# The opening of a fused Fourier transform and feed-forward kernel: one table in another queue, x ahead of w1, fewer warm-ups, weight loads behind the first relayout

## The chip, the core and the metric

The kernel runs on one core of a Trainium2 chip. The core has a matrix engine (PE, with its weight loads listed as PEld), a vector engine (DVE), a scalar engine (ACT), a general engine (POOL) and a sync engine (SP) that issues most of the transfers. ACT and POOL can issue transfers too. Each engine works through its own instructions in order; semaphores between them tell when a tile is ready. Sixteen DMA engines move the data between device memory and the core's SBUF.

The metric is the time of one execution on the device in microseconds (us), lower is better.

## What is computed

```python
def _attn_ref(x):                       # x: (8, 3136, 256), float32
    X = np.fft.fft(x, axis=1)
    X = np.fft.fft(X, axis=2)
    return X.real.astype(np.float32)

def _moe_ref(x, g_ln, w_ch1, w_ch2):    # w_ch1: (256, 1024), w_ch2: (1024, 256)
    mu = np.mean(x, axis=-1, keepdims=True)
    var = np.mean((x - mu) ** 2, axis=-1, keepdims=True)
    xn = (x - mu) / np.sqrt(var + 1e-06) * g_ln
    ch = np.maximum(xn @ w_ch1, 0.0) @ w_ch2
    return (x + ch).astype(np.float32)

# out = _moe_ref(_attn_ref(x), ...)
```

x is float32. The weights w_ch1 and w_ch2 arrive as 64-bit floats, which the kernel reads as pairs of 32-bit words and turns into 32-bit floats itself.

## The kernel before

The 3136 positions of a batch are split as 49 x 64. Per batch, **step1** is the transform over the 64: seven pieces (`step1(b, i)`), each a matmul group against the table tu (`tu_s`) on tiles that were folded into sums first (`fold_zw`, on DVE for batch 0). `step1_ends` does the columns that the fold leaves out; it reads `ends` (POOL). Each piece is copied out of PSUM by ACT (L267) and stored to scratch in device memory (`store1`, L271). When all seven pieces of a batch are stored, **relayout** (L278) reads them back with the 49 on the partitions; batch 0 does so in three parts (groups 0 to 4, 4 to 8, 8 to 16). **step2** (L311) is the transform over the 49, against the table tab (`tab_s`) and, for the first group, tz (`tz_s`). ACT casts its result to the rounded high part ckh (L332), DVE makes the low part ckl (L336).

Then come 49 chunks of 256 positions with their mirror images, 8 steps each: `moe1_a` (matmuls with w1, L356, and sum and difference on ACT and DVE, L361 to L363), `moe1_b` (ReLU and split into high and low part, L370 and L371) and `moe2` (matmuls with w2, L406). Each product is made of three passes of rounded high and low parts. The transform over the 256 columns is folded into w1 (`transform_w1`, L576) in the opening, and the residual goes through its own small matmuls (L431).

The weights are converted in pieces. Four pieces of w1 (w1_0 to w1_3) and four of w2 share the same four buffers: `load_w2(n)` writes where w1_n was, so it comes after the conversion of w1_n has read it. A conversion has an ACT part, `convert_z` (L531), and DVE parts, `convert_m` (L523, L525) and `convert_b` (L536, L538); `convert_b` needs both. `finish_w1` (L566) and `finish_w2` (L598) put the parts together; `split_w2` makes high and low part of w2 (ACT L542, POOL L543); `round_w1` (L584) and `rest_w1_copy` (L594), both on ACT, make those of w1.

The order of the work of PE, ACT, DVE and POOL, and in the opening of SP too, is the order of the lines from L685 on: every engine takes its own instructions in the order in which they stand there. In the opening ACT has, behind the step1 copies, `convert_z` of the w1 pieces, the two casts of `round_w1(0)`, `convert_z` of w2_0 and of w2_1, `rest_w1_copy(0)`, `round_w1(1)`, the cast of `split_w2(0)` and then the ckh casts of step2. PE has step1, the transforms of w1, fifteen warm-up matmuls, step2 for the first two pairs of groups and then `moe1_a(0)`. The eight warm-ups at the very start (L683, L691) multiply zeros; three of them are in float32, which PE runs as two passes each, and five in bfloat16.

The transfers of one engine form one queue, and a semaphore of a small set tells when a transfer has landed. An issue also waits until the transfer that used its semaphore before has landed.

Of the kernel before, what the change touches and what calls it, by code (L numbers as in the profile page):

```python
# [146 lines left out]
def tile_kernel(ctx: ExitStack, tc: tile.TileContext, x, g_ln, w1, w2, tu, tab, tz, ty, tw, out):  # L147
    nc = tc.nc
# [15 lines left out]
    tu_s = const.tile([128, 388], F32, name="tu_s")  # L164
    tab_s = const.tile([KP, 2, HALF], F32, name="tab_s")
# [13 lines left out]
    def load_x(b, i):  # L179
        in_order(nc.sync.dma_start(xs[:, i], x[b, i]))  # L180
# [17 lines left out]
    def fold_zw(b, i, eng):  # L198

        if i > 3 and b == 0:  # L200
            t = weights.tile([128, HW], F32, tag="h_hi", name=f"zw{b}_{i}", bufs=4)
        else:
            t = work.tile([128, 2 * 256], F32, tag="zw", name=f"zw{b}_{i}", bufs=3)
        z, w = (t[:, 256 * h:256 * h + 256].rearrange("p (s d) -> p s d", s=2) for h in range(2))
        zw[b, i] = z, w
        a, c = xs[:, i, 0:2], xs[:, i, 2:4]
        eng.tensor_tensor(out=z, in0=a[:, :, 1:129], in1=c[:, :, 255:127:-1], op=ALU.add)
        eng.tensor_tensor(out=w, in0=a[:, :, 255:127:-1], in1=c[:, :, 1:129], op=ALU.add)
# [72 lines left out]
    gb = group_bounds()  # L281
# [247 lines left out]
    def convert_z(key, wp):  # L529
        high, e = conv[key][:2] if key in conv else convert_e(key, wp)  # L530
        nc.scalar.activation(e, high.bitcast(F32), AF.Copy, scale=2.0 ** -112)  # L531

    def convert_b(key):
        high, e, f = conv[key]
        e = e.bitcast(I32)
        nc.vector.tensor_scalar(out=e, in0=e, scalar1=3, scalar2=0x7F800000,  # L536
                                op0=ALU.logical_shift_left, op1=ALU.bitwise_and)
        nc.vector.scalar_tensor_tensor(out=e, in0=high, scalar=-0x80000000, in1=e,  # L538
                                       op0=ALU.bitwise_and, op1=ALU.bitwise_or)
# [15 lines left out]
    def load_w2(n):  # L555
        wp = w1p[n]
        nc.sync.dma_start(wp.rearrange("p (f d) -> p f d", f=2), w2v[:, 2 * n:2 * n + 2])
        w2p.append(wp)
# [120 lines left out]
    def warm_up(n, zeros):  # L679

        pw = psum.tile([128, 2 * D], F32, tag="fft", name="pw")
        for i in range(n):
            nc.tensor.matmul(pw, zeros[:, :128], zeros, start=True, stop=True)  # L683

    E = mybir.EngineType  # L685
    with tc.manual_schedule(engines={E.PE, E.Activation, E.DVE, E.Pool}):
        with tc.manual_schedule(engines={E.SP}):
            nc.vector.memset(one, 1.0)
            for t in (warm, warm_h):
                nc.vector.memset(t, 0.0)  # L690
            for n, t in ((3, warm), (5, warm_h)):  # L691
                warm_up(n, t)
            nc.scalar.dma_start(g_s, g_ln.rearrange("(i p) -> p i", p=128))
            nc.scalar.activation(one, one, AF.Sqrt)
            nc.sync.dma_start(tu_s, tu)
            load_x(0, 0)
            load_x(0, 1)
            load_w1(0)
            for i in (2, 3, 4):
                load_x(0, i)  # L700
            load_w1(1)
            for i in (5, 6):
                load_x(0, i)
            load_w1(2)
            load_w1(3)
            nc.sync.dma_start(tw_all, tw)
            nc.gpsimd.memset(zmu, 0.0)
            nc.gpsimd.memset(masked, 0.0)
            ends(0, 0, 6)
            fold_zw(0, 0, nc.vector)  # L710
            step1(0, 0)
            nc.vector.tensor_scalar_mul(g_s, g_s, 2.0 ** -20)
            fold_zw(0, 1, nc.vector)
            convert_z("w1_0", w1p[0])
            step1(0, 1)
            convert_m("w1_0", w1p[0])
            fold_zw(0, 2, nc.vector)
            step1(0, 2)
            convert_b("w1_0")
            load_w2(0)  # L720
            nc.sync.dma_start(tab_s[:, :, :gb[4]], tab[:, :, :gb[4]])
            nc.sync.dma_start(tz_s, tz)
            step1_ends(0, 0, 6)
            for i in range(3):
                store1(0, i, nc.scalar if i % 2 else nc.gpsimd)
            ends(0, 6, 10)
            fold_zw(0, 3, nc.vector)
            step1(0, 3)
            convert_z("w1_1", w1p[1])
            fold_zw(0, 4, nc.vector)  # L730
            step1(0, 4)
            finish_w1(0)
            step1_ends(0, 6, 10)
            store1(0, 3, nc.scalar)
            store1(0, 4, nc.gpsimd)
            ends(0, 10, NS)
            convert_m("w1_1", w1p[1])
            fold_zw(0, 5, nc.vector)
            step1(0, 5)
            convert_z("w1_2", w1p[2])  # L740
            convert_b("w1_1")
            load_w2(1)
            fold_zw(0, 6, nc.vector)
            step1_ends(0, 10, NS)
            store1(0, 5, nc.scalar)
            step1(0, 6)
            store1(0, 6, nc.gpsimd)
            finish_w1(1)
            convert_z("w1_3", w1p[3])
            convert_m("w1_2", w1p[2])  # L750
            convert_b("w1_2")
            finish_w1(2)
            relayout(0, 0, 4)
            relayout(0, 4, 8)
            load_w2(2)
            nc.sync.dma_start(tab_s[:, :, gb[4]:gb[8]], tab[:, :, gb[4]:gb[8]])
            relayout(0, 8, 16)
            nc.scalar.copy(minus, tw_all[:, 512:])
            transform_w1(0, 0)
            transform_w1(0, 1)  # L760
            round_w1(0)
            convert_m("w1_3", w1p[3])
            convert_b("w1_3")
            load_w2(3)
            nc.sync.dma_start(ty_s, ty)
            nc.sync.dma_start(tab_s[:, :, gb[8]:], tab[:, :, gb[8]:])
            for i in range(NU):
                load_x(1, i)
            finish_w1(3)
            transform_w1(1, 0)  # L770
            rest_w1(0)
            convert_z("w2_0", w2p[0])
            convert_z("w2_1", w2p[1])
            rest_w1_copy(0)
            transform_w1(1, 1)
            round_w1(1)
            convert_m("w2_0", w2p[0])
            convert_b("w2_0")
            f = finish_w2(0)
            split_w2(0, f)  # L780
            convert_m("w2_1", w2p[1])
            convert_b("w2_1")
            warm_up(15, warm_h)
            step2(0, "m")
            step2(0, "hl")
            step2(1, "m")
            step2(1, "hl", 0)
            f = finish_w2(1)
            moe1_a(0, ((1, 0), (0, 0), (0, 1)))
            split_w2(1, f)  # L790
            step2(0, "f")
            moe1_a(1, ((1, 0), (0, 0), (0, 1)))
            rest_w1(1)
            moe1_b(0)
            moe1_a(2)
            moe1_b(1)
            moe1_b(2)
            moe1_a(3)
            rest_w1_copy(1)
            step2(1, "f")  # L800
            convert_a("w2_2", w2p[2])
            step2(1, "hl", 1)
            moe2(0)
            moe1_b(3)
            moe1_a(4)
            convert_b("w2_2")
            f = finish_w2(2)
            nc.gpsimd.tensor_scalar(out=neg, in0=ty_s[:, 1, 129:130], scalar1=2.0, scalar2=-1.0,
                                    op0=ALU.mult, op1=ALU.add)
            moe2(1)  # L810
            step2(2, "m")
            moe1_b(4)
            split_w2(2, f)
            moe1_a(5)
            step2(2, "hf")
            step2(2, "l")
            convert_a("w2_3", w2p[3])
            moe2(2)
            add_late(6, convert_b, "w2_3")
            add_late(6, lambda: w2f.append(finish_w2(3)))  # L820
            add_late(7, lambda: split_w2(3, w2f.pop()))
            add_late(14, split, t1_hi, t1_lo, tu_s[:, 0:128])

        main.append(True)
        lag, last = 3, 8 * NCH
        for s in range(6, last):
            moe1_b(s - 1)
            moe1_a(s)
            for fn, args in late.get(s, ()):
                fn(*args)  # L830
            moe2(s - lag)
            for fn, args in after.get(s, ()):
                fn(*args)
        moe1_b(last - 1)
        inverse_std(LC)
        moe2(last - 3)
        for i, side in ((0, 0), (1, 0), (0, 1), (1, 1)):
            for t in (last - 2, last - 1):
                moe2(t, ((i, side),))
            finish_last(i, side)  # L840
# [18 lines left out]
```

## Time and profile before

| what | us |
|---|---|
| median of 3 runs | 989.09 (988.50 to 989.29) |
| the profiled execution | 990.76 |
| its span, first to last instruction | 989.0 |
| PE busy | 979.8 (99%) |
| DVE busy | 814.3 (82%) |
| ACT busy | 535.2 (54%) |
| POOL busy | 248.6 (25%) |
| moved by DMA in the span | 92.12 MB, mean 93 GB/s |

The span leaves out 1.8 us of the profiled execution that lie before the first and behind the last instruction. A group of instructions is named by its engine, its line in the kernel and what it writes and reads, so "PE ab L356" is a matmul of line 356 into the tile ab. In the lists in order of time the first column is the start in us from the beginning of the span and the second the length; what stands in brackets is the idle time of the engine just before and what ended it. The lists of transfers give the size and the median time from issue to landing. "DMA share" is the busy share of the sixteen DMA engines. w1p_all is the buffer that holds the raw pieces of w1 and, later, of w2, so "w1p_all<-w" is a load of either; "scratch<-s" is a store of step1 and "s<-scratch" a relayout.

### The profile page before, as it was taken

How to read it: one execution, taken by the hardware profiler on the slowest of the kernel's cores; microseconds unless marked ns; L12 is line 12 of the kernel's file. 1: busy time of each engine (PE TensorE's matmuls, PEld its weight loads, DVE VectorE, ACT ScalarE, POOL GpSimd, SP SyncE). 2: the span in 40 equal slices, each digit the busy share in tenths (PEclk: the TensorE clock that was granted, in tenths of full speed). 3: DMA queues.
4: the chain of work that ended last, by engine and by line, in shares of the span. 5: the costliest groups of instructions: out<-in, count | busy, mean ns of one | idle time of the engine just before them, and what ended most of it. 6: DMA issues, size and time to landing. Idle time of an engine off the chain costs nothing.

```text
span 989.0 us, 22057 instructions
## 1 busy us (share of the span) xinstructions
PE 979.8 (99%) x8436; PEld 964.9 (98%) x8436; DVE 814.3 (82%) x2190; ACT 535.2 (54%) x1416; POOL 248.6 (25%) x278
## 2 busy tenths in 40 slices
PE   9899999999999999999999999999999999999998
PEld 6699999999999999999999999999999999999998
DVE  6688887888888888888888888888888888888887
ACT  3556555555555555555555556555555554555553
POOL 2156433223422332322342234223322300000000
PEclk9999999999999999999999999999999999999999
DMA  9943352214221252111521242211311113100101
GB/s 345 251 169 115 105 178 86 86 55 139 87 94 57 76 152 96 63 67 65 172 86 55 86 139 87 96 55 69 114 49 39 55 49 91 44 23 22 44 23 44
DMA packets 41529, 92.12 MB, mean 93 GB/s; under 512 B 4176, under 2 KB 18704, under 8 KB 40528
## 3 DMA queue, kind: packets, MB, share of 16 engines
q1 hardware_dynamic: 40016, 88.87, 27.2%
q8 instruction: 67, 1.10, 0.5%
q0 software_dynamic: 320, 1.05, 0.3%
q10 hardware_dynamic: 1088, 0.79, 0.2%
q14 instruction: 38, 0.31, 0.1%
HBM read 50.32 MB, written 40.37 MB: 92 GB/s over the span
## 4 chain that ended last, share of the span: by engine, by line
PE 93%; DVE 3%; ACT 1%; DMA 1%; issue 0%; SPq 0%; DVEq 0%; ACTq 0%
PE acc L406 51%; PE ab L356 26%; PE ps L311 6%; PE psy L431 4%; PE ps L263 3%; DVE h_lo L371 1%; PE pw L683 1%; DMA scratch<-s 1%; PE ps L255 1%; PE ps L257 1%; DVE h L362 1%; DVE h L363 1%; DMA s<-scratch 0%; ACT h_hi L370 0%; ACT asb L361 0%
## 5 line engine op out<-in xcount | busy, mean ns | idle before, releaser
L406 PE MATMUL acc<-w_hi,h_lo 128*128 128x256 f32 x1568 | 433.4, 276 | 0.2 <-DVE h_lo L371 0.2
L406 PE MATMUL acc<-w_lo,h_hi 128*128 128x256 f32 x1568 | 433.2, 276 | 0.0
L406 PE MATMUL acc<-w_hi,h_hi 128*128 128x256 f32 x1568 | 433.1, 276 | 0.0
L371 DVE SCALAR_TENSOR_TENSOR h_lo<-h,h_hi 128x512 fp32r<-128x512 f32 x392 | 293.5, 749 | 140.4 <-ACT h_hi L370 137.7
L370 ACT ACTIVATE h_hi<-h 128x512 fp32r<-128x512 f32 x392 | 250.0, 638 | 291.6 <-DVE h L363 291.6
L406 PEld LDWEIGHTS acc<-w_hi,h_lo 128*128 128x128 f32 x1568 | 294.5, 188 | 0.6 <-DVE h_lo L371 0.4
L406 PEld LDWEIGHTS acc<-w_hi,h_hi 128*128 128x128 f32 x1568 | 294.4, 188 | 0.0
L406 PEld LDWEIGHTS acc<-w_lo,h_hi 128*128 128x128 f32 x1568 | 294.4, 188 | 0.0
L356 PE MATMUL ab<-ckl,w_hi 128*128 128x256 f32 x768 | 218.0, 284 | 1.6 <-DVE h L363 1.5
L356 PE MATMUL ab<-ckh,w_lo 128*128 128x256 f32 x768 | 212.8, 277 | 0.5 <-ACT ckh L332 0.4
L356 PE MATMUL ab<-ckh,w_hi 128*128 128x256 f32 x768 | 212.3, 276 | 0.0
L225 POOL TENSOR_TENSOR fl<-f,fh 128x512 fp32r<-128x512 f32 x49 | 64.0, 1306 | 504.6 <-ACT fh L219 493.9
L362 DVE TENSOR_TENSOR h<-asb,ab 128x256 f32<-128x256 f32 x384 | 158.5, 413 | 1.6 <-ACT asb L361 1.5
L363 DVE TENSOR_TENSOR h<-asb,ab 128x256 f32<-128x256 f32 x384 | 158.5, 413 | 0.0
L356 PEld LDWEIGHTS ab<-ckl,w_hi 128*128 128x128 f32 x768 | 144.3, 188 | 2.7 <-ACT w_hi L542 1.5
L356 PEld LDWEIGHTS ab<-ckh,w_lo 128*128 128x128 f32 x768 | 144.3, 188 | 0.9 <-ACT ckh L332 0.5
L356 PEld LDWEIGHTS ab<-ckh,w_hi 128*128 128x128 f32 x768 | 144.2, 188 | 0.0
L361 ACT COPY asb<-ab 128x256 f32<-128x256 f32 x384 | 138.3, 360 | 9.4 <-PE ab L356 2.2
L267 ACT COPY s<-ps 128x508 f32<-128x508 f32 x56 | 32.8, 585 | 65.3 <-PE ps L263 51.2
L311 PE MATMUL ps<-tab_s,s 112*128 112x98 f32 (+1 forms) x512 | 65.5, 273 | 1.8 <-DMA s<-scratch 1.8
L311 PEld LDWEIGHTS ps<-tab_s,s 112*128 112x128 f32 x512 | 61.8, 191 | 2.3 <-issue 2.3
L332 ACT CAST ckh<-ps 128x392 fp32r<-128x392 f32 (+49 forms) x112 | 39.7, 355 | 42.0 <-PE ps L311 41.8
(108 smaller groups left out, 979.5 us busy)
## 6 DMA issues: line engine op xcount, KB each, us to landing
xs<-x SPq DMA_DIRECT2D x56, 512.0 KB, 4.1
out<-o SPq DMA_DIRECT2D x96, 256.0 KB, 2.0
scratch<-s SPq DMA_DIRECT2D x49, 256.0 KB, 2.3
s<-scratch SPq DMA_DIRECT2D x7, 1792.0 KB, 10.0
w1p_all<-w SPq DMA_DIRECT2D x8, 512.0 KB, 8.2
scratch<-s POOLq DMA_DIRECT2D x4, 256.0 KB, 6.4
s<-scratch SPq DMA_DIRECT2D x2, 448.0 KB, 5.2
s<-scratch SPq DMA_DIRECT2D x1, 896.0 KB, 11.0
```

Of the source, the lines that this page charges most:

```text
L225: nc.gpsimd.tensor_tensor(out=lo, in0=f, in1=hi.bitcast(F32), op=ALU.subtract)
L267: nc.scalar.copy(s[:, :, :, :127], ps[:, :, :, :127])
L311: nc.tensor.matmul(ps[:, h, k0 - base:k1 - base], s2[b][:KP, g, 128 * h:128 * h + 128], tab_s[:, h, k0:k1], start=(h == 0 and g == 2 * j), ...
L332: nc.scalar.copy(hi, src)
L356: nc.tensor.matmul(pt, wt[wi][:, j, fs], ch[xi][:, j, :w], start=(n == 0), stop=(n == 2))
L361: nc.scalar.copy(asb[:, :w], pa)
L362: nc.vector.tensor_tensor(out=h[:, :w], in0=asb[:, :w], in1=pb, op=ALU.add)
L363: nc.vector.tensor_tensor(out=h[:, w:], in0=asb[:, :m], in1=pb[:, :m], op=ALU.subtract)
L370: nc.scalar.activation(h_hi, h, AF.Relu)
L371: nc.vector.scalar_tensor_tensor(out=h_lo, in0=h, scalar=0.0, in1=h_hi.bitcast(F32), op0=ALU.max, op1=ALU.subtract)
L406: nc.tensor.matmul(acc[c, i][:, side], hs[xi][:, h0:h0 + 128], ws[wi][:, f], start=(f == 0 and side == 0 and n == 0), stop=(f == 7 and n = ...
L431: nc.tensor.matmul(ps[:, j, :n], ck[:, j], ty_s[:, j, :n], start=(j == 0), stop=True, skip_group_check=True)
```

## The change

Only the order of the opening for batch 0 and the queues of two transfers are changed, and three warm-ups are dropped; no arithmetic is.

- Two float32 and three bfloat16 warm-ups stand in place of three and five.
- The load of tu is issued by ACT, ahead of that of g_ln, in place of SP.
- x(0,0), x(0,1) and x(0,2) are loaded ahead of w1_0, in place of the first two.
- The first part of tab and tz are loaded right behind tw, in place of behind w2_0.
- The load of w2_0 moves behind the first relayout and that of w2_1 behind the second.
- On DVE, the folds of x stand ahead of the conversions beside them; on ACT, `convert_z` of w1_2 moves behind the last store.
- The store of the last step1 piece is issued by ACT in place of POOL.

```diff
-            for n, t in ((3, warm), (5, warm_h)):
+            for n, t in ((2, warm), (3, warm_h)):
                 warm_up(n, t)
+            nc.scalar.dma_start(tu_s, tu)
+            load_x(0, 0)
             nc.scalar.dma_start(g_s, g_ln.rearrange("(i p) -> p i", p=128))
             nc.scalar.activation(one, one, AF.Sqrt)
-            nc.sync.dma_start(tu_s, tu)
-            load_x(0, 0)
-            load_x(0, 1)
+            for i in (1, 2):
+                load_x(0, i)
             load_w1(0)
-            for i in (2, 3, 4):
+            for i in (3, 4):
                 load_x(0, i)
             load_w1(1)
             for i in (5, 6):
...
             load_w1(2)
             load_w1(3)
             nc.sync.dma_start(tw_all, tw)
+            nc.sync.dma_start(tab_s[:, :, :gb[4]], tab[:, :, :gb[4]])
+            nc.sync.dma_start(tz_s, tz)
             nc.gpsimd.memset(zmu, 0.0)
             nc.gpsimd.memset(masked, 0.0)
             ends(0, 0, 6)
...
             step1(0, 0)
             nc.vector.tensor_scalar_mul(g_s, g_s, 2.0 ** -20)
             fold_zw(0, 1, nc.vector)
+            step1(0, 1)
+            fold_zw(0, 2, nc.vector)
             convert_z("w1_0", w1p[0])
-            step1(0, 1)
             convert_m("w1_0", w1p[0])
-            fold_zw(0, 2, nc.vector)
             step1(0, 2)
-            convert_b("w1_0")
-            load_w2(0)
-            nc.sync.dma_start(tab_s[:, :, :gb[4]], tab[:, :, :gb[4]])
-            nc.sync.dma_start(tz_s, tz)
+            fold_zw(0, 3, nc.vector)
             step1_ends(0, 0, 6)
             for i in range(3):
                 store1(0, i, nc.scalar if i % 2 else nc.gpsimd)
+            convert_b("w1_0")
             ends(0, 6, 10)
-            fold_zw(0, 3, nc.vector)
             step1(0, 3)
+            fold_zw(0, 4, nc.vector)
             convert_z("w1_1", w1p[1])
-            fold_zw(0, 4, nc.vector)
             step1(0, 4)
             finish_w1(0)
             step1_ends(0, 6, 10)
             store1(0, 3, nc.scalar)
             store1(0, 4, nc.gpsimd)
             ends(0, 10, NS)
+            fold_zw(0, 5, nc.vector)
             convert_m("w1_1", w1p[1])
-            fold_zw(0, 5, nc.vector)
             step1(0, 5)
-            convert_z("w1_2", w1p[2])
-            convert_b("w1_1")
-            load_w2(1)
             fold_zw(0, 6, nc.vector)
             step1_ends(0, 10, NS)
             store1(0, 5, nc.scalar)
+            convert_b("w1_1")
             step1(0, 6)
-            store1(0, 6, nc.gpsimd)
+            store1(0, 6, nc.scalar)
+            convert_z("w1_2", w1p[2])
             finish_w1(1)
             convert_z("w1_3", w1p[3])
             convert_m("w1_2", w1p[2])
             convert_b("w1_2")
             finish_w1(2)
             relayout(0, 0, 4)
+            load_w2(0)
             relayout(0, 4, 8)
+            load_w2(1)
             load_w2(2)
             nc.sync.dma_start(tab_s[:, :, gb[4]:gb[8]], tab[:, :, gb[4]:gb[8]])
             relayout(0, 8, 16)
```

## The prediction

> **What bounds the kernel now.** I read the chain that ended last first, in order of time, because the change touches only the first 32 us of a 989 us program (columns: start us, length us, what).
>
> ```profile
> 1.49 5.50 PE pw L683 x6
> 7.04 1.44 PE pw L683 x5
> 8.47 0.43 PE ps L255 x2
> ...
> 22.32 0.59 ACT s L267
> 22.92 0.29 issue
> 23.20 6.65 DMA scratch<-s
> ...
> 30.06 4.57 DMA s<-scratch
> ...
> 37.02 0.27 ACT ckh L332
> 37.29 0.04 issue
> 37.34 1.08 PE ab L356 x6
> ...
> 64.07 0.94 PE ab L356 x6
> ```
>
> The reader sees three stretches. Up to 22.3 us PE sets the pace: warm-ups, then seven step1 tiles without a gap. From 22.3 to 37.3 us it is a relay: copy, last store (issued 23.20, landed 29.85), first relayout (30.06 to 34.63), step2, cast, first channel matmul. From 37.3 on it is DVE, ACT and then PE work that never stops again, so a shift of the first channel matmul (moe1_a(0), L356 at 37.34) is carried to the end one for one. The price of the change is the shift of that one event. The stages behind it, by windows (PE, PEld, DVE, ACT, POOL busy, granted clock, DMA share, GB/s):
>
> ```profile
> 0.00:4.00 4.00, 2.51 (x3) 1.17 (x4) 0.82 (x3) 1.49 (x2) 0.64 (x6) 1.00 0.41 99
> 4.00:22.00 18.00, 17.94 (x79) 13.43 (x78) 12.85 (x29) 5.48 (x13) 3.60 (x7) 1.00 1.02 397
> 28.00:30.00 2.00, 2.00 (x7) 0.71 (x7) 0.89 (x2) 0.00 (x0) 0.00 (x0) 1.00 0.17 61
> 38.00:44.00 6.00, 5.40 (x40) 4.61 (x38) 4.77 (x12) 4.92 (x13) 1.29 (x1) 1.00 1.03 279
> 44.00:64.00 20.00, 19.02 (x158) 18.35 (x156) 18.07 (x44) 11.14 (x32) 8.43 (x11) 1.00 0.69 239
> ```
>
> The DMA engines are full from 4 to 22 us (share 1.02) at 397 GB/s. DVE with 18.07 of 20 us between 44 and 64 has little slack to win a late start back.
>
> **What stands beside the chain.** The chain shows only what came last. ACT works in program order, and between the opening and the first cast of step2 (ckh, L332) it has the weight work:
>
> ```profile
> 30.91 0.69 ACT L531 ACTIVATE ew<-w1p_all 128x512 f32<-128x512 f32 x1 [3.90 <-DMA w1p_all<-w]
> 31.50 1.06 ACT L594 CAST w_lo<-psw 128x512 fp32r<-128x512 f32 x2
> 32.44 1.09 ACT L584 CAST w_hi<-psw 128x512 fp32r<-128x512 f32 x2
> 33.40 0.65 ACT L542 CAST w_hi<-fw 128x512 fp32r<-128x512 f32 x1
> 36.13 0.48 ACT L332 CAST ckh<-ps 128x390 fp32r<-128x390 f32 x1 [2.08 <-PE ps L311]
> ```
>
> The first row is convert_z of w2_1. It waited 3.90 us for the load of w2_1, and everything behind it, ckh too, stood in its queue. Once w2_1 was there ACT needed until 34.05 and then idled 2.08 us for step2. **That 2.08 us is the only distance between the chain and a second limit, the landing of w2_1**, and w2_1 is a load which the change moves.
>
> **The parts.**
>
> *Opening.* Six passes of fp32 warm-up took 5.50 us (0.92 each) and five bf16 ones 1.44 (0.29). Two fp32 warm-ups are four passes, 3.7 us from 1.49; three bf16 take 0.9, or 1.3 if the clock is still low. PE is free at 6.1 to 6.5 in place of 8.47. The data must be there too: x(0,0) is now the first on SP's queue and tu goes by ACT's.
>
> ```profile
> xs<-x SPq DMA_DIRECT2D x1, 512.0 KB, 4.7
> 5.92 0.43 DVE L207 TENSOR_TENSOR zw<-xs 128x256 f32<-128x256 f32 x1 [4.21 <-DMA xs<-x]
> 6.26 0.42 DVE L208 TENSOR_TENSOR zw<-xs 128x256 f32<-128x256 f32 x1
> 25.05 0.75 DVE L566 SCALAR_TENSOR_TENSOR gw<-fw,g_s,ew 128x512 f32<-128x512 f32 x1
> ```
>
> The tile issued at 1.20 landed after 4.7, at 5.9. It was issued behind tu and now goes out 0.45 earlier, so it lands at about 5.4 and its fold ends by 6.3. step1 starts near 6.3, 2.0 to 2.2 earlier; if PE's clock comes up only at 7 us, as its slow passes before 7 suggest, 0.4 to 0.7 of that is lost. The tiles land 1.3 apart (0.52 MB at 397 GB/s) and PE needs 1.72 each (four rows of 0.43), so PE isn't starved; x(0,2) moves ahead of w1_0 and helps. The reordered folds and conversions on DVE run beside PE. Last step1: 20.4 to 20.8 in place of 22.3; ACT's copy 0.59 more, and the last store (now on ACT's queue, without POOL's 0.29) goes out at about 21.0 in place of 23.2. convert_z of w1_2 is now queued behind that store on ACT; the two remaining w1 folds on DVE then end near 26.6 (five conversion steps of 1.1 and 0.75 behind 21.7), 0.8 later than the last row above (25.05 + 0.75), hidden behind relayout(0,0,4).
>
> *Landing of the last store.* By 22 us, 4 x 99 + 18 x 397 = 7.54 MB have moved. Ahead of and with the last store now stand tu 0.20, seven x 3.67, four w1 2.10, tw 0.33, table 0.35, tz 0.02 and seven stores 1.84: 8.50 MB, since both w2 loads (1.05 MB) are gone. At 397 GB/s that is 22 + 0.96/0.397 = 24.4, less about 0.5 for the earlier start. The same sum for store 5 of before (8.39 MB) gives 24.1 and it landed at 24.9, so 0.7 of lag is added: 24.6. A second way: the row of store 5, issued by ACT at 21.01 into the same full engines,
>
> ```profile
> scratch<-s ACTq DMA_DIRECT2D x1, 256.0 KB, 3.9
> scratch<-s POOLq DMA_DIRECT2D x1, 256.0 KB, 6.6
> ```
>
> gives 21.0 + 3.9 = 24.9. I take 24.7 (bounds 23.3 to 26), 5.1 earlier than 29.85. The 28 to 30 window above, a DMA share of 0.17, shows that the second row is no matter of bandwidth: one straggling part kept the store open.
>
> *Relayouts and w2.* SP issues the first relayout 0.2 later, at 24.9. Loads of one queue came in order here; issued at 30.06, 30.44 and 30.97:
>
> ```profile
> s<-scratch SPq DMA_DIRECT2D x1, 448.0 KB, 4.6
> s<-scratch SPq DMA_DIRECT2D x1, 448.0 KB, 5.9
> w1p_all<-w SPq DMA_DIRECT2D x1, 512.0 KB, 7.0
> w1p_all<-w SPq DMA_DIRECT2D x1, 512.0 KB, 7.2
> ```
>
> They landed at 34.63, 36.30 and 37.97. So the relayout needs 4.6, and its two followers 1.7 each. Relayout(0,0,4) lands at 29.5, 5.1 earlier. **But w2_1 is now fourth in that queue, behind relayout, w2_0 and relayout**: 24.9 + 7.9 for three + 1.7 = 34.5. Before, by the last row, it landed at 23.61 + 7.22 = 30.83. It becomes 3.7 later. Bounds: at the full 397 GB/s of the opening the four (1.97 MB) take 5.0 plus 0.9 to the first byte, 30.8; with the late bound of the store and 0.5 more per load, 36.8. I hold to 34.5, the nearest rows being the same transfers in the same queue.
>
> *The end of the path.* From w2_1's landing to the end of ACT's weight work took 3.2 us (30.83 to 34.05), hardly any of it waiting. Both ckh casts follow at once, ending 3.7 after the landing, and DVE's two ckl (0.96 together, the first behind the first ckh) end 4.3 after it: 38.8. Now they end at 36.65 + 0.96 = 37.61:
>
> ```profile
> 36.65 0.96 DVE L336 TENSOR_TENSOR ckl<-ps,ckh 128x390 fp32r<-128x390 f32 x2 [3.57 <-ACT ckh L332]
> ```
>
> **Sum**: 38.8 - 37.6 = +1.2 us. step2 itself is early (2.2 us of work behind the warm-ups, below; PE is done by about 34) but its casts wait on ACT. The break-even is w2_1 at 33.3. The profiled execution took 990.76 us with a span of 989.0; the runs shown have the median 989.09. I add to the median: **990.3**. The later loads (w2_2, tables, second batch) land some 1.5 to 2 us earlier and nobody on the chain waits for them. table and tz sooner: the first step2 matmul waited for the relayout and not for them (its row stands with rival B), so by themselves they are worth nothing; their bytes are in the sum.
>
> **The rivals.**
>
> *A: the gain comes through (faster).* If the four transfers run at the opening's rate, w2_1 lands at 30.8 as now, ckh follows ACT's work at about 34, the second one ends at 34.5 in place of 37.29, with PE's step2 ending at about 34: -2.8, 986.3. For it: the relayout's 0.46 MB in 4.6 us are 100 GB/s, so it is not bandwidth and w2_0 might overlap it. Against it: the window 38 to 44, all of the same queue's loads, has DMA share 1.03 at just 279 GB/s.
>
> *B: PE goes cold (slower).* PE finishes its fifteen warm-ups and step2, then stands until ckh:
>
> ```profile
> 28.68 1.02 PE L576 MATMUL psw<-gw,tw_all 128*128 128x512 f32 x2
> 29.53 3.40 PE L683 MATMUL pw<-warm_h 128*128 128x512 bf16 x15
> 34.77 0.66 PE L311 MATMUL ps<-tab_s,s 112*128 112x99 f32 x4 [1.83 <-DMA s<-scratch]
> 35.44 1.54 PE L311 MATMUL ps<-tab_s,s 112*128 112x98 f32 x12
> ```
>
> Before, the hole was 1.83 us and the clock held. Now the transforms end near 28.4 (the last needs the w1 fold of 26.6 and four passes of 0.43), the warm-ups 3.3 later near 31.7, step2 (34.77 to 36.98) near 34, and moe1_a(0) starts at 38.3: a hole of over 4 us. The trace shows what a cold PE is: 0.92 a pass at the start against 0.43 (28.68 to 29.53 for two) later; the granted clock reads 1.00 throughout and doesn't tell. It took 5.5 us of work at the start (1.49 to 7.04) to come up. In 38 to 44 PE was busy 5.40 of 6 us; at half speed that work overruns by up to 4, with the clock back midway by about 1.8: 1.2 + 1.8, **992.1**. It decides from a hole that is long enough; no row shows how long. [...]
>
> *C: the relayout queue is slower still (slower).* If w2_0's 2 KB rows slow the second relayout to the first one's 4.6, w2_1 lands at 36 or later: +2.7 or more, 991.8.
>
> *D: the change does not move the store.* If its landing is held by a straggler as in 28 to 30 us, by 2 us or so, relayout and w2_1 both slip: up to +3.
>
> **How the numbers follow.** Forecast 990.3 (w2_1's wait takes the store's place, result between -1.3 and +2.0): 0.53. A: 0.13. B: 0.21. C and D together: 0.13, most of it over +2. The measurement can tell about 0.2% (2 us) from no change. Faster by that is A alone, 0.13. Slower is B and most of C and D, 0.32. The same is 0.55. The range reaches down into A and up past B and C: 987.2 to 992.5.
>
> **What the new profile would show.** Right: the last store on ACT's queue at about 21 and landed by 25; relayout(0,0,4) landed near 29.5; the row of ACT L531 for w2_1 at about 34.5 with a wait on the load; L332 without a wait for PE ps, directly behind L542; the releaser of PE L356 an ACT or DVE cast near 38.5; the chain from 25 to 38 going through the load of w. Wrong: L332 still waiting for PE ps; w2_1 landed before 32; moe1_a passes at about 0.24 apart in place of 0.12 (then B).

## The result, and the profile after

| what | before | after |
|---|---|---|
| median of 6 runs each, us | 989.26 (988.50 to 990.65) | 996.10 (995.08 to 997.16) |
| the profiled execution | 990.76 | 996.43 |
| its span | 989.0 | 994.7 |
| mean granted clock of PE in it | 1.000 | 0.996 |

The change made the kernel slower, by less than 1%: 1.0067 of the time before, 95% interval 1.0055 to 1.0080. The forecast was 990.3, the range 987.2 to 992.5; the time lies 3.6 us above the range.

First the chain that ended last, after the change, in order of time (start, length, what):

```profile
1.19 7.17 DMA g_s<-g_ln
8.93 0.70 PE ps L255 x2
...
22.25 4.28 DMA scratch<-s
...
28.68 9.58 DMA w1p_all<-w
...
42.06 3.13 PE ab L356 x12
45.86 0.70 PE ab L356 x6
```

It begins with a transfer of which the prediction says nothing, g_s (7.17 us for 1 KB). It then goes where the prediction sent it, through the last store and the load of w2_1 (9.58), but the first channel matmul starts at 42.06, not at 38.3, and its passes are slow: 12 in 3.13 us (0.26 each), where the next six take 0.12 each.

The beginning of that chain and its end, in the list of instructions (the bracket is the idle time just before and what ended it):

```profile
4.96 0.42 DVE L207 TENSOR_TENSOR zw<-xs 128x256 f32<-128x256 f32 x1 [3.25 <-DMA xs<-x]
8.38 0.17 DVE L715 TENSOR_SCALAR g_s<-g_s 128x2 f32<-128x2 f32 x1 [2.65 <-DMA g_s<-g_ln]
8.46 0.42 DVE L207 TENSOR_TENSOR zw<-xs 128x256 f32<-128x256 f32 x1
8.93 0.70 PE L255 MATMUL ps<-zw,tu_s 128*128 128x256 f32 x2 [1.36 <-DVE zw L207]
...
35.07 0.69 ACT L531 ACTIVATE ew<-w1p_all 128x512 f32<-128x512 f32 x1 [8.40 <-DMA w1p_all<-w]
38.34 0.67 ACT L531 ACTIVATE ew<-w1p_all 128x512 f32<-128x512 f32 x1 [2.58 <-DMA w1p_all<-w]
...
40.81 0.65 ACT L542 CAST w_hi<-fw 128x512 fp32r<-128x512 f32 x1
41.33 0.68 ACT L332 CAST ckh<-ps 128x390 fp32r<-128x390 f32 x2
```

Three things are to be seen. x(0,0) was folded at 4.96, a full microsecond sooner than before, and then DVE stood still for 2.65 us, waiting for g_s; the fold of x(0,1) waits behind that and PE behind the fold (1.36). The second row of ACT L531 is w2_1's, at 38.34 behind a wait for the load: the releaser that the prediction named, 3.8 us later than it said. And ckh (L332) follows L542 directly, without a wait for step2, as forecast.

The transfers, with the time from issue to landing:

```profile
tu_s<-tu ACTq DMA_DIRECT2D x1, 194.0 KB, 4.4
g_s<-g_ln ACTq DMA_DIRECT2D x1, 1.0 KB, 7.2
s<-scratch SPq DMA_DIRECT2D x1, 448.0 KB, 4.8
w1p_all<-w SPq DMA_DIRECT2D x1, 512.0 KB, 9.6
```

Before, this row of g_s read

```profile
g_s<-g_ln ACTq DMA_DIRECT2D x1, 1.0 KB, 3.2
```

Last, the windows after the change (PE, PEld, DVE, ACT, POOL busy, granted clock, DMA share, GB/s):

```profile
4.00:22.00 18.00, 15.99 (x75) 12.41 (x73) 11.99 (x27) 5.39 (x13) 3.83 (x7) 1.00 1.00 384
35.30:38.70 3.40, 0.56 (x6) 0.40 (x4) 2.97 (x6) 0.82 (x2) 0.00 (x0) 1.00 1.09 299
38.70:45.50 6.80, 3.44 (x14) 3.21 (x15) 3.97 (x9) 4.86 (x14) 1.86 (x2) 0.50 1.03 232
45.50:48.90 3.40, 3.40 (x27) 3.04 (x25) 3.11 (x7) 2.61 (x7) 0.71 (x1) 1.00 1.06 220
```

PE was busy 15.99 of the 18 us of the opening (17.94 before). From 35.86, the end of step2, to 42.06 it had nothing to do, and for 6.8 us from 38.7 on the granted clock is 0.50: rival B.

### The profile page after: what moved, and what is told of

Read it like the earlier page. It is cut to its first block, busy times and chain, and to the rows that moved or that the text cites. A ratio compares the mean times of both kernels' runs of the same rounds, so it can differ in the third digit from the quotient of the medians.

```text
span 994.7 us, 22049 instructions
## 1 busy us (share of the span) xinstructions
PE 979.2 (98%) x8431; PEld 965.3 (97%) x8432; DVE 814.6 (82%) x2190; ACT 535.1 (54%) x1416; POOL 248.2 (25%) x277
## 4 chain that ended last, share of the span: by engine, by line
PE 91%; DVE 3%; DMA 2%; ACT 2%; issue 1%; POOL 0%; SPq 0%; ACTq 0%; DVEq 0%; POOLq 0%
PE acc L406 51%; PE ab L356 26%; PE ps L311 5%; PE psy L431 4%; PE ps L263 3%; DMA w1p_all<-w 1%; DVE h_lo L371 1%; DMA g_s<-g_ln 1%; DVE h L362 1%; DVE h L363 1%; ACT h_hi L370 0%; DMA scratch<-s 0%; PE ps L255 0%; PE ps L257 0%; ACT asb L361 0%
## 5 line engine op out<-in xcount | busy, mean ns | idle before, releaser
L332 ACT CAST ckh<-ps 128x392 fp32r<-128x392 f32 (+49 forms) x112 | 39.6, 356 | 39.7 <-PE ps L311 39.5
```

The lines of the kernel that those rows point to most:

```text
L332: nc.scalar.copy(hi, src)
```

## The experiments

Each time below is a median, and each ratio is against runs of the kernel before on the same chip (medians 989.42 to 989.73).

### The move of the w2 loads: undone, and alone

`e1_w2_back` is the changed kernel with both loads back ahead of the relayouts.

```diff
             convert_b("w1_0")
+            load_w2(0)
...
             convert_b("w1_1")
+            load_w2(1)
...
             relayout(0, 0, 4)
-            load_w2(0)
             relayout(0, 4, 8)
-            load_w2(1)
```

> The changed kernel with one part undone: the loads of w2_0 and w2_1 stand at their old places ahead of the relayouts. Theory Q (the loss is the place of w2_1 in SP's queue, since ACT's convert_z of w2_1 stands ahead of everything that step2 needs): w2_1 lands no more than 2 us after the first relayout was issued, moe1_a(0) starts before 38.5 us (42.06 in the changed kernel), the hole in PE's work shrinks under 3 us and the clock holds; 987 to 990 us. Rival G (the loss is the opening: DVE held by the load of g_s, SP by its semaphore, the last store landed at 26.5): the time stays at 993 or more. Rival C (PE's clock alone): like Q here, as the hole is gone.

`e2_w2_alone` is the kernel before with this move and nothing else: the inverse edit, made in before.

> The kernel before with one part of the change alone: both loads of w2 moved behind the first and the second relayout. Theory Q: the last store lands at 28 to 29.9, w2_1 some 11.5 us after the first relayout's issue as in the changed kernel, near 40 or later; moe1_a(0) near 44, and the clock falls in the hole: 995 to 999 us. Rival G: the place of the loads costs nothing, 989.

Measured: e1 989.76, ratio 1.0002 (0.9993 to 1.0011); e2 994.64, ratio 1.0051 (1.0039 to 1.0063). Without the move the rest of the change is worth nothing that can be measured; the move alone costs 5.0 us. The expectation of e2 missed on the way, since store and w2_1 came sooner than it said, and its time lies just under the range. In the chain of e2

```profile
1.49 4.58 PE pw L683 x6
...
22.10 4.12 DMA scratch<-s
26.85 5.90 DMA w1p_all<-w
...
35.74 0.67 ACT ew L531
...
38.87 0.56 ACT ckh L332 x2
39.47 1.86 PE ab L356 x6
```

w2_1 landed at 35.66, 9.2 us behind the issue of the relayout at 26.42, and the rest follows as the prediction has it: ACT's work (3.1 us), two ckh, ckl, first channel matmul at 39.47, which is 2.1 later than before. The load in this chain is w2_0's, landed at 32.76: convert_z of w2_1 (ACT L531, 35.74) began 0.08 us behind its own load, but right behind DVE's last step for w2_0 (35.73). The two w2 loads hold step2's casts almost equally here.

The store landed at 26.21 in this kernel too, 3.6 sooner than before, though none of the opening's other edits is in it: it took 4.12 in place of 6.65, and was issued 1.1 sooner. The load of w2_0 is no longer ahead of it and that of w2_1 no longer 0.4 us behind it; which of this shortened it was not tried. Here too the store stayed open while the DMA engines had little to do: from 25.0 to 26.0 the DMA share was 0.06 or less.

The earlier issue has another source, and it matters for the account below. PE's work up to step1 is the same in e2 and in before, but the six passes of fp32 warm-up took 4.58 here and 5.50 in before's profiled execution, and step1 started at 7.19 in place of 8.31. By the trace's records the clock came up at 4.99 here and at 7.47 there. Before's profiled execution is one of a late clock. The six passes, step1 and the store's issue each moved by 0.9 to 1.1 us with it, in this one pair of executions.

### The clock: a bridge of warm-ups

`e3_bridge` puts 28 bfloat16 warm-ups into the hole between step2 and the first channel matmul of the changed kernel, in PSUM banks that are free there (`warm_up` is given the name of the banks).

```diff
             step2(1, "hl", 0)
+            warm_up(28, warm_h, "ab")
             f = finish_w2(1)
             moe1_a(0, ((1, 0), (0, 0), (0, 1)))
```

> The changed kernel with 28 more bfloat16 warm-ups (of zeros, 0.216 us each) between step2 for the first two pairs of groups and moe1_a(0), in a PSUM bank of their own, so that PE isn't idle from 35.9 to 42.1 us. Theory Q: the granted clock stays at 1.00, moe1_a(0) starts where it did (42.1) and the time falls by about 1.0 us (the stretch from 42.06 to 69.76 took 1.0 longer than its counterpart from 37.34 to 64.07): 995. Rival C: most of the 6.8 us is the clock: 991 or less.

Measured: 995.34, ratio 1.0057 (1.0045 to 1.0069). The clock is 1.00 throughout in all five executions. The window in which it had been at half speed is here

```profile
38.70:42.10 3.40, 3.40 (x18) 1.72 (x17) 1.96 (x4) 2.26 (x6) 1.27 (x1) 1.00 1.01 262
42.10:45.50 3.40, 2.92 (x21) 2.35 (x21) 1.98 (x6) 2.48 (x8) 1.28 (x1) 1.00 1.04 271
```

So the cold clock isn't where most of the loss is: the medians differ by 0.8 us, and the intervals of the two kernels overlap. But this is not its price. The bridge ended too late: the chain goes through its last 24 warm-ups to 42.09, and moe1_a(0) starts 0.8 us behind the second ckh cast (40.96), where after and e4 have 0.05. What the clock costs and what the bridge costs stand against each other here.

### The wait for g_s: undone, and made worse

`e4_g_later` moves one DVE instruction of the changed kernel, the scaling of g_s, from ahead of the second fold to the place where it is first needed. No transfer moves.

```diff
             step1(0, 0)
-            nc.vector.tensor_scalar_mul(g_s, g_s, 2.0 ** -20)
             fold_zw(0, 1, nc.vector)
...
             step1(0, 4)
+            nc.vector.tensor_scalar_mul(g_s, g_s, 2.0 ** -20)
             finish_w1(0)
```

> The changed kernel with the scaling of g_s on DVE moved from ahead of the second fold to ahead of its first use (finish_w1(0)), so that DVE doesn't wait for the load of g_s. Theory Q: the second step1 tile starts about 1.3 us earlier (at 7.6), the last store goes out up to 1.4 us earlier, and since the stores share full DMA engines with the rest the landing moves by 0 to 1.4 us and with it everything behind: 994.5 to 996. Rival G: this wait is most of the loss, 992 or less.

Measured: 992.64, ratio 1.0035 (1.0022 to 1.0047), 3.5 us below the changed kernel, whose interval lies wholly above this one. The time is near rival G's and far below the 994.5 to 996 expected. Its profiled execution runs through the stations of the prediction within half a microsecond:

| station | predicted | e4 | after |
|---|---|---|---|
| last store landed | 24.7 | 24.25 | 26.53 |
| first relayout landed | 29.5 | 29.62 | 31.58 |
| w2_1 landed | 34.5 | 34.61 | 38.26 |
| second ckl ends | 38.8 | 38.99 | 42.64 |

and ends 1.9 us later than these stations explain, with a cold clock. That they agree so closely is in part luck of the execution: its clock came up at 4.66 us, as after's did at 4.56. e8 and e11 (below) have the opening of e4 up to the last store's issue; in their profiled executions the clock came up at 7.51 and 7.69, and the store went out at 22.41 and 22.45 (21.06 in e4) and landed at 26.89 and 26.65. The chain and the windows of e4:

```profile
34.69 0.68 ACT ew L531
...
37.82 0.39 ACT ckh L332
...
38.24 0.77 DVE ckl L336 x2
...
39.05 2.50 PE ab L356 x10
```

```profile
32.00:35.40 3.40, 3.34 (x22) 2.21 (x21) 3.26 (x7) 1.39 (x3) 0.00 (x0) 1.00 1.05 319
35.40:38.80 3.40, 1.01 (x8) 0.76 (x7) 2.14 (x5) 2.97 (x7) 0.90 (x1) 1.00 1.08 270
38.80:42.20 3.40, 3.27 (x15) 2.96 (x13) 1.88 (x6) 1.90 (x6) 1.30 (x2) 0.50 1.01 266
```

The hole is only 2.4 us long here (36.03 to 38.42), and yet the clock fell.

`e12_g_first` keeps the scaling where the change has it and puts the load of g_ln ahead of that of tu in ACT's queue.

```diff
+            nc.scalar.dma_start(g_s, g_ln.rearrange("(i p) -> p i", p=128))
             nc.scalar.dma_start(tu_s, tu)
             load_x(0, 0)
-            nc.scalar.dma_start(g_s, g_ln.rearrange("(i p) -> p i", p=128))
```

> The changed kernel with the load of g_ln issued ahead of that of tu on ACT's queue, everything else as the change has it. The scaling of g_s stays ahead of the second fold. If its 4-byte packets were late because they queue behind tu among the loads of x: g_s lands by 5 us (8.36 in the changed kernel), DVE and SP don't wait for it, and the time falls as in e4, to 991.5 to 993.5. If the packets are slow wherever they stand: g_s lands after 7 us and the time stays at 995 to 997.

Measured: 996.76, ratio 1.0072 (1.0059 to 1.0084): no gain. The transfers of its opening:

```profile
tu_s<-tu ACTq DMA_DIRECT2D x1, 194.0 KB, 7.2
g_s<-g_ln ACTq DMA_DIRECT2D x1, 1.0 KB, 5.1
```

g_s landed at 5.83 and nobody waited for it, but tu, now the second of ACT's queue, landed at 8.45, and step1, which can't begin without it, started at 8.58. PE had waited 2.01 us for it, the clock fell to 0.50 from 9.66 to 13.07, and the last store went out at 25.34 only. So the wait changed hands, and neither expectation fits in full. Whichever of the two went second in ACT's queue landed at 8.4 us or later (tu at 8.45 here, g_s at 8.36 to 9.20 in the eleven runs that have the change's order).

### The two together, and what then limits

`e5_back_g` is e1 with the edit of e4; `e6_back_g_8warm` is e5 with 8 in place of 15 warm-ups ahead of step2; `e9_tw_early` is e6 with the load of tw ahead of w1_2; `e10_tw_tab` is e9 with the first part of tab and tz back behind w2_0.

```diff
-            warm_up(15, warm_h)
+            warm_up(8, warm_h)
```

```diff
+            nc.sync.dma_start(tw_all, tw)
             load_w1(2)
             load_w1(3)
-            nc.sync.dma_start(tw_all, tw)
```

```diff
-            nc.sync.dma_start(tab_s[:, :, :gb[4]], tab[:, :, :gb[4]])
-            nc.sync.dma_start(tz_s, tz)
...
             load_w2(0)
+            nc.sync.dma_start(tab_s[:, :, :gb[4]], tab[:, :, :gb[4]])
+            nc.sync.dma_start(tz_s, tz)
```

> Both loads of w2 back ahead of the relayouts (as in e1) and the scaling of g_s moved behind the folds (as in e4); the rest of the change stays. Theory Q: with both causes gone the rest of the opening is left, the first relayout lands near 32.3 (33.05 in e1), the fifteen warm-ups end near 33.5 and moe1_a(0) starts near 36.2 (37.34 before): 987.5 to 989.3 us, a little under the kernel before. Rival G (the opening itself is worse in another way too): 990 or more.

> As the run e5 with eight in place of fifteen warm-ups ahead of step2, which would otherwise end after the first relayout has landed. Theory Q: PE waits for the relayout again, moe1_a(0) starts 0 to 1.5 us earlier than in e5 and the clock holds, since no stretch of 3.4 us is mostly idle: 986.5 to 989. If the warm-ups were not in the way: as e5.

> The run e6 with the load of tw moved ahead of w1_2 and w1_3. In e6 PE stood still from 20.3 to 22.6 us until tw had landed, and in the profiled execution the granted clock was 0.5 from 23.3 to 26.7 us; its executions with a mean clock of 1.00 took 988.0 to 989.3 us, those under it 989.2 to 993.8. Theory Q with the clock: tw lands before 20 us, PE doesn't stop, the clock is 1.00 in nearly every execution and the median is 987.5 to 988.6, under the kernel before. Rival: the spread of e6 has another cause, and stays; 989 or more.

> The run e9 with the first part of tab and tz back behind the load of w2_0, as before the change. In the changed kernel the earlier place in SP's order did not bring tab forward: its issue waited for the landing of the second store (21.46 us, 22.10 before) and held the queue behind it. Theory Q: w2_0 is issued by 16 us, w2_1 and the first relayout land 0 to 1.5 us earlier than in e9, and the time is that of e9 or up to 1 us less: 986.8 to 988.6. Rival: tab's place matters by itself and this is slower than e9 by 0.5 or more.

| kernel | median | ratio to before (interval) | last store landed | relayout landed | first channel matmul |
|---|---|---|---|---|---|
| before | 989.26 | | 29.85 | 34.63 | 37.34 |
| e1 | 989.76 | 1.0002 (0.9993 to 1.0011) | 28.57 | 33.05 | 37.12 |
| e5 | 989.42 | 1.0000 (0.9991 to 1.0009) | 24.61 | 32.84 | 35.94 |
| e6 | 989.24 | 1.0000 (0.9988 to 1.0011) | 24.18 | 32.75 | 36.30 |
| e9 | 988.25 | 0.9993 (0.9982 to 1.0003) | 25.61 | 31.34 | 34.05 |
| e10 | 988.42 | 0.9992 (0.9983 to 1.0000) | 25.47 | 31.28 | 33.99 |

The times of e5 and e6 lie just above what was expected, those of e9 and e10 inside it. In the profiled executions the first channel matmul of e10 is 3.3 us sooner than before's, and the time is 3.3 lower (990.76 and 987.50); the medians differ by 1.0 only, since before's profiled execution lies above its median and e10's below. What held each back differs. In e1 it was PE's own queue: the chain has

```profile
31.22 3.25 PE pw L683 x15
34.52 0.69 PE ps L311 x4
...
37.12 1.07 PE ab L356 x6
```

and the relayout, landed at 33.05, had to wait for the warm-ups. In e5 the store landed 4 us sooner than in e1, and the relayout 0.2 sooner: issued at 24.80 it took 8.0 us behind two loads of w2, with the DMA engines full (share 1.00 at 271 GB/s from 24.8 to 32.8). In e6 PE waited for tw:

```profile
22.62 4.54 PE L576 MATMUL psw<-gw,tw_all 128*128 128x512 f32 x6 [2.30 <-DMA tw_all<-tw]
```

and the clock fell after it:

```profile
19.90:23.30 3.40, 1.10 (x4) 0.46 (x4) 1.75 (x4) 2.10 (x4) 0.00 (x0) 1.00 1.06 391
23.30:26.70 3.40, 3.40 (x6) 1.32 (x5) 3.30 (x6) 0.00 (x0) 0.00 (x0) 0.50 0.95 244
```

The executions of e6 go from 988.03 to 993.75. Those of clock 1.00 took 988.03 to 989.27, the others, with a mean clock of 0.995 to 0.998, 989.2 to 993.75. So half of them lost their clock, which was to hold. With tw early (e9) the wait is gone in the profiled execution, and the chain goes through DMA again:

```profile
20.91 4.70 DMA scratch<-s
25.76 5.58 DMA s<-scratch
31.47 0.66 PE ps L311 x4
```

The medians of e9 and e10 are the lowest, 1.2 and 1.0 us under before's, but not clear of it: the interval of e9 takes in 1, that of e10 ends at it. The clock still falls now and then: three of e9's twelve executions had a mean clock of 0.997 and took 990.5 to 991.8. Whether tab stands early or late makes no difference that can be measured; w2_0 didn't go out by 16 us in e10 either, but at 20.59.

### Three that missed

`e7_g_bridge10` is e4 with ten warm-ups as a bridge, to price its cold clock.

```diff
             step2(1, "hl", 0)
+            warm_up(10, warm_h, "ab")
             f = finish_w2(1)
```

> The run e4 (the loads of w2 where the change puts them, g_s scaled late) with ten bfloat16 warm-ups of zeros between step2 and moe1_a(0), 2.2 us of work in a hole of 2.4. The clock's price by the profiled executions: in e4 the end came 1.9 us later than the start of moe1_a(0) explains. Theory Q: clock at 1.00, moe1_a(0) where it was (38.4), the time falls by 1.0 to 1.9 us to 990.7 to 991.7. If the clock cost nothing here: 992.6 as e4.

Measured: 992.57, ratio 1.0037 (1.0021 to 1.0052), no better than e4. The clock held over the hole, but fell from 23.11 to 26.53, behind the wait of PE for tw. And the bridge, begun at 37.40 behind a later step2, ended late again: moe1_a(0) started at 39.21, 0.8 us behind the second ckh cast (38.44). So the price of the cold clock in e4 was not isolated.

`e8_act_order` is e4 with the conversion of w2_1 moved behind the first channel matmul on ACT and DVE, so that ckh no longer queues behind it.

```diff
             convert_z("w2_0", w2p[0])
-            convert_z("w2_1", w2p[1])
...
-            convert_m("w2_1", w2p[1])
-            convert_b("w2_1")
...
-            f = finish_w2(1)
             moe1_a(0, ((1, 0), (0, 0), (0, 1)))
+            convert_z("w2_1", w2p[1])
+            convert_m("w2_1", w2p[1])
+            convert_b("w2_1")
+            f = finish_w2(1)
```

> The run e4 with the conversion of w2_1 (convert_z on ACT; convert_m, convert_b and finish_w2 on DVE) moved behind moe1_a(0); the loads stay behind the relayouts. Theory Q (ACT's program order ties step2's casts to the landing of w2_1): ckh no longer waits for w2_1, moe1_a(0) starts at about 36.4 (38.4 in e4) with w2_1 landing as late as there, the clock holds; 2.2 us of DVE work that was hidden moves into the busy stretch behind it: 990 to 991.5 us. Rival D (the queue of DMA engines itself is the limit, whatever ACT does): moe1_a(0) stays at 38 or later, 992.6.

Measured: 993.87, ratio 1.0046 (1.0033 to 1.0058). The wait moved, it didn't go. In the list of ACT's instructions

```profile
34.00 0.68 ACT L531 ACTIVATE ew<-w1p_all 128x512 f32<-128x512 f32 x1 [8.10 <-DMA w1p_all<-w]
...
36.92 0.62 ACT L542 CAST w_hi<-fw 128x512 fp32r<-128x512 f32 x1 [0.30 <-DVE fw L598]
37.44 0.64 ACT L332 CAST ckh<-ps 128x390 fp32r<-128x390 f32 x2
```

the second ckh now ends 1.1 us behind the landing of w2_1 (36.94) where e4 has 3.8 between them, so it no longer queues behind that load. But it queues behind w2_0's conversion in the same way, w2_0 landed only at 33.92, and the work that was moved stands on DVE and ACT behind the first channel matmul, where the clock fell a second time (0.50 from 45.06 to 51.89). This profiled execution is the slowest of its five (996.20) and one of a late first clock; how far the landings at 33.92 and 36.94, 2.0 and 2.3 later than in e4, come from that wasn't separated.

`e11_w21_second` is e4 with w2_0 back ahead of the relayouts and w2_1 directly behind the first of them.

```diff
             convert_b("w1_0")
+            load_w2(0)
...
             relayout(0, 0, 4)
-            load_w2(0)
-            relayout(0, 4, 8)
             load_w2(1)
+            relayout(0, 4, 8)
```

> The run e4 with the load of w2_0 back at its old place and that of w2_1 directly behind the first relayout, so that w2_1 is second in that queue in place of fourth. Theory Q: w2_1 lands 6 to 8 us after the first relayout's issue (10.2 in e4) and moe1_a(0) starts at 35.8 to 37 us (38.4 in e4), whichever of w2_1 and the relayout is later; 988.8 to 990.3 us. Rival D (the sum of the bytes ahead of step2 is what counts, not the order): w2_1 near 34.6 as in e4 and 992 or more.

Measured: 992.00, ratio 1.0023 (1.0014 to 1.0032). w2_1 landed 7.6 us behind the issue of the relayout (10.2 in e4), as expected. But the store landed at 26.65 (24.25 in e4), and so w2_1 landed at 34.48, where e4 had it at 34.61, and moe1_a(0) started at 38.31. The late store isn't the work of w2_0, which went out at 23.27, behind the store's issue at 22.45: e8, without any w2 load there, has a store as late (22.41, landed 26.89), and both are executions of a late first clock. That the median isn't clear of e4's either, 992.00 and 992.64 with overlapping intervals, is not explained by this one trace. Ten of its eleven executions lost clock (0.997 or 0.998); the eleventh took 989.71.

## Why the prediction was wrong, step by step

The whole account, by profiled executions (each against before's 990.76, with the first channel matmul at 37.34):

| kernel | time | of it, later start of moe1_a | rest |
|---|---|---|---|
| after | +5.67 | +4.72 | +0.95 (half clock) |
| e2, w2 moved alone | +3.88 | +2.13 | +1.75 (half clock) |
| e3, after with a bridge | +4.88 | +4.40 | +0.48 (clock 1.00, bridge late) |
| e4, after without the wait for g_s | +3.02 | +1.08 | +1.94 (half clock) |
| e1, after without the w2 move | -0.22 | -0.22 | 0.00 (clock 1.00) |

A rest of half a us can have another source than the clock, as e3 shows. The medians differ by more: 6.8 for after, 5.0 for e2. Before's profiled execution lies 1.5 us above the median of its six runs; by comparison with e2 some 1.1 of that is its late clock ahead of step1, an estimate from one pair of executions. The prediction added a difference of profiles to the median and so carried this over: its +1.2 was counted from a late before. Of the 5.8 us between forecast and median, 3.5 go with the wait for g_s (after against e4). In the 2.3 that e4 keeps, the cold clock (1.9) and the late base (1.7 above the median to which the sum was added) stand against the 1.1 by which e4's own profiled execution lies above its median.

**The opening: the step that failed.** "The reordered folds and conversions on DVE run beside PE" leaves out the one DVE instruction that the change doesn't move. The scaling of g_s stands ahead of the second fold in both kernels. Before, its load was alone in ACT's queue, landed at 3.93 and nobody waited. The change puts tu ahead of it in that queue; it landed at 8.36, DVE stood 2.65 us, PE 1.36, and the last store went out at 22.25, not 21.0. The prediction costed tu's move as a gain for x and never asked what had become second in ACT's queue. SP stood too: the load of x(0,5) uses the semaphore of g_s, waited 2.9 us for its landing and went out at 8.37. PE itself started step1 at 5.68, earlier than the 6.3 of the forecast; without the wait (e4) the last step1 tile ended at 20.41, inside the predicted 20.4 to 20.8. The wait is worth 3.5 us in the medians where w2_1 queues behind the relayout (after against e4), and about 0.3, less than the runs can tell, where it doesn't (e1 against e5). That 1.36 us of PE become 3.5 at the end is not followed through: against e4 the store went out 1.2 later, took 1.1 longer, and w2_0 came 1.1 later still (below).

**The landing of the last store** was right as a mechanism (early, on ACT's queue) and in size in e4, where the wait is gone: 24.25; it was 26.53 after, just outside the bounds of 23.3 to 26. That tab comes sooner was costed at nothing, and so it was, for a reason that the prediction didn't have: its issue waited 6.9 us for the landing of the second store, whose semaphore it uses, and went out at 21.46.

**The queue of the relayouts** was the right mechanism: the chain goes through the load of w2, ckh follows L542, and moe1_a follows ckl. Four transfers were to take 9.6 us from the issue of the first to the landing of w2_1. They took 9.2 in e2, 10.2 in e4 and 11.5 after. So after had 1.8 from the store and 1.9 from this term, 3.8 in all at w2_1, and the same at ckl. The excess stands in one of the four: w2_0 landed 3.4 behind the first relayout after, 2.3 in e4 and 1.5 in e2, where the prediction had 1.7; the other two took 1.1 to 1.7 each in all three. It is not the change's opening alone that does it: e3, with the same opening, has 1.9 there and 10.1 for the four. What slows w2_0 wasn't found.

**The end of the path**, 4.3 us from w2_1's landing to the second ckl, was 4.4 in after, in e2 and in e4.

**The clock (rival B)** was given 0.21, the author's estimate, with no row for how long a hole it takes; it happened in the profiled execution of every kernel with the w2 move and no bridge. The prediction reckoned with a hole of over 4 us. In e4 one of 2.4 us was enough: PE was busy 1.01 of the 3.40 us from 35.40 to 38.80, and the clock was 0.50 in the 3.40 us behind them. By the forecast's own figures the two belonged together: whenever w2_1 lands at 34.5 the hole is there, so B's chance should have been nearly that of the forecast, and 992.1 its likeliest time; e4 took 992.64. The price of 1.8 agrees with the 1.75 and 1.94 of e2 and e4, each one pair of executions; in the changed kernel the rest was 0.95. No run isolates the price, since both bridges held moe1_a(0) back themselves.

**The rivals A, C and D.** A (the four at the opening's rate) is refuted by all kernels with the move. C and D come near what happened, w2_1 at 36 or later and the store 2 us late, but not by the mechanisms named: it is w2_0 that was slow and not the second relayout, and the store was issued 1.2 late and took 4.28 in place of 3.7.

## What to carry to other kernels

When a transfer is moved into another queue, look at every transfer that now stands behind it and for the first instruction that reads each, in program order: a 1-KB load read by one small instruction held up DVE by 2.65 us, PE by 1.36 and, through its semaphore, SP by 2.9 here. A load put behind a relayout was late by the queue ahead of it here (w2_1, fourth in the queue, landed 9.2 to 11.5 us behind the issue of the first relayout), so price it by its landing against what waits for it, and remember that the bytes only change sides: with both w2 loads ahead of the relayouts w2_1 landed at 31.05 and the first relayout at 32.84 (e5), with both behind at 34.61 and 29.62 (e4). Before a profile is used as the base of a sum, see whether its execution is a late one. And where an estimate opens a hole on PE such as those here (2.4 us in e4, 6.2 after, each with the clock at 0.50 behind it), the fall of the clock belongs to the forecast and not to a rival.

## What the runs showed of the hardware

**The stretches at clock 0.50 lasted 3.41 or 6.83 us in the opening, and PE had work in what lay ahead of them.** They go from 38.69 to 45.52 after, 39.13 to 42.54 in e2, 38.79 to 42.20 in e4 and 23.29 to 26.70 in e6. From the clock's first rise to its first fall 34.13 us passed in after, e2 and e4, 30.72 in e8 and 17.07 in e6. In the 3.4 us just ahead of the fall PE was busy 0.56 (after), 1.01 (e4) and 1.10 us (e6). In the 3.4 us of before that held its hole it was busier, and its clock held:

```profile
31.40:34.80 3.40, 1.57 (x9) 0.55 (x6) 1.64 (x3) 2.65 (x6) 0.66 (x1) 1.00 0.91 245
```

The busy time alone doesn't decide: before kept its clock with 1.57 us, nine warm-ups of 512 columns, and e12 lost it with 1.92 us of 3.41 (36.97 to 40.38), eighteen passes of step2 of 50 to 99 columns. What else counts wasn't tried. The clock first came up between 4.56 us (after) and 7.69 (e11), and one kernel lost its clock in some executions and kept it in others: of e6's twelve, six had a mean clock of 1.00 and six of 0.995 to 0.998. The prediction said that the granted clock doesn't tell; it did, with 0.50 in the stretches above.

**One small transfer took 3.2 us in one place and 7.2 in another.** g_s, 1 KB in elements of 4 bytes, took 3.2 us as the first of its queue before the change, 5.1 as the first in e12, where tu stands behind it, and 7.2 as the second after the change. In the stretch from 4.0 to 8.4 us after the change the queues moved (packets, MB, share)

```profile
q1 hardware_dynamic: 368, 1.33, 86.7%
q10 hardware_dynamic: 312, 0.04, 6.1%
```

that is, nearly as many packets of ACT's queue (q10) as of SP's (q1), with 3% of the bytes. Why g_s took longer there is not shown.
